# An S4 convolution and a gated GLU on one core: the hand-kept order of all work replaced by another

## The chip, the cores and the metric

The kernel runs on one core of a Trainium2 chip. The metric is device time in microseconds; the time of a kernel is the median of several runs. The profiles are of one execution each and count from the first to the last instruction (the span).

## What is computed

The input u has 2048 rows of 512 channels. Two branches work on it and are mixed by a gate per row:

```python
g = sigmoid((x * gate_w).sum(-1, keepdims=True))
# a: S4 convolution along the rows, one filter per channel
P = exp((dt * A)[:, :, None] * l)                  # 512 channels, 128 states, 2048 steps
K = einsum("dn,dnl,dn->dl", Cc, P, dB).real
a = irfft(rfft(u padded) * rfft(K padded))[:L] + u * Dskip
# b: gated GLU
b = (sigmoid(x @ w_gate) * (x @ w_up)) @ w_down    # 512 -> 1792 -> 512
return g * a + (1 - g) * b
```

## The kernel before

TensorE does two kinds of work. The wide products are the GLU: `gups` (line 1130, 1344 products of 128x512) are the hidden layer, and `dps` (line 1202, 672 products) the way down. Each float32 operand is split into a high and a low part, so three products stand for one. The small products are the convolution, done as a transform in two steps. They come in visits, each of one name:

- `ups` (line 742, 8 visits): first step of the transform of u. ScalarE copies the result to `evu`, and SyncE's queue writes it to `a_u` in memory (line 782).
- `kps` (line 653, 16 visits): the filter K, from the tables `B` (last operation on VectorE: line 590) and `T` (line 611). `B` and `T` have one buffer each. ScalarE copies the result to `kst`, and VectorE adds Dskip to it (line 670).
- `wps` (line 683, 8 visits): first step of the transform of K from the `kst` of two kps. ScalarE copies to `kev` (line 692), and SyncE writes `a_k` (line 698), one array for each half of the channels.
- `s2u`, `s2k` (lines 849 and 876, 8 visits each): second step, on `au` and `ak`, 1 MB each, read back from `a_u` and `a_k` (lines 819 and 828), with constants `wwu`, `wwk`. VectorE multiplies the two.
- `ips` (line 914, 8 visits) goes back; its result goes to `b_s` through `ev` (line 936).
- `fps` (line 990, 8 visits) is the last step, on `b_in` (line 977). The names `parts` are pieces of buffers that the first stage no longer needs and that hold au, ak, b_in and the sums in the second half.

The channels are done in two halves. The second half's s2u and s2k can't begin before the last kps and wps are done and written to memory. `sps` (line 409) is one product that spreads the gate's weights. The FFN's rows are done in two halves of 1024 as well; wide products remain until the end and are what TensorE does while the other work waits for memory.

Every strand of work is a generator that yields one step at a time: engine, cost, function, dependencies. `Plan.run` takes the next letter of the string `ORDER` (line 67 on; a letter stands for a kind of strand and an engine), and issues the next step of that kind. The string therefore sets the order of the instructions on every engine and on the DMA queues of SyncE and GpSimd; each engine works off its own in that order. The plan also keeps times of its own from cost figures (for a transfer so many KB, for a TensorE visit so many microseconds). They decide nothing on the chip but which free buffer is taken, and the semaphores come from the dependencies of the tiles.

Of the kernel before, what the change touches and what calls it, by code (L numbers as in the profile page):

```python
# [32 lines left out]
P = 128  # L33
L, D, F = 2048, 512, 1792
# [32 lines left out]
ORDER = (
    "ABEjDkhidDhEdHGDhjikddEjikIEDjkhddiEjkKZatatatdEdayzjktbFlDhiEjdyzAdkdddDhiEmedjkFydduzDhiLLMlNymMCOOPGDhdiydQOFRSdldmQE"
    "QQbZzezddQOTRyzejQWyddkWTWOWyTEjEzWdEWd0eeeTd1dOPQWEzWcWddjyyyUVVWkW0eeZdejdkvxxxW0exzvcLZx1xzWxaUeeaxzOEdUUyQWUWzFa1dWv"
    "xyQdRSTadWkExxxEyddRWtWX0YTtztQjvzTTUdtbxxxyseexeddQyyOVdVbZdUUzUUkRuj0e1leedScZQXyz0YdWzjTR1WkdseWGnovxedymWzjWeTdyddTk"  # L70
    "LTzdWkWzWWWxyzvyx1EUWEWdz0eedxFxy1xFxcedFZWjVzkWddldmWlmyyVUzUdxalmtUvxxaxx0ejvaxpqdaeeEUzyRSTdxqzje02yEtWddeeeeRTTEtWkd"
    "WWX0Y2tdrybxErTUseeededbMZzVNxMdOO02edejyeeVUPQOkUydUdQzUjRkScXZzEQz0YQQO2dTRseejQWydeneWTrjWWWWdkWdWWzvyzWxyeddzdWTv0ee"
    "eWTWdU1yEzky0eeeecdZOVVxoEWx0eeeeWzddWx2OPQdvjr2kOQQUExFUxly2UUzLRyduxSTFxkvWRmdWpxydadtzWXjkTTzFa0YlmxyTQlxFdylmUtsdzmd"
    "xeeyezadtjVxkQzxyLzeOVUExaEdj0qeUete2Uqer2r0dURyESTeeezyXed0YQb2jksR2dTbWzWedeeeTjZkckWdTy0eeWeWeWvxxxxEdUdV20eeZeexvWrx"
    "xxxWdcWVnW2WW0eejeezyWUUWUU2zWRSdyvx0eeeFFzoTdeWdRFWxlvpmrkdyzWWX2ldDDmD0YTyzTTxl2hdmiqsydehehUdMNizMOOeLxViPQOVUUUUdRSQ"
    "dx0DeQyzQXe2e0QOTRyddYQW2zWWsnodWqxrrrrOWTWyzThWOPWeedQdpWedTiWUxyWWOdqDDxWzWqrrr0edeVeyWzrVUUWUU0ddhyQDhQezdfRSf4566yzW"
    "hTRe2Wdd2e0QidyDhWeXiTieeizdy0YTTUQzfOf89%VVUUUdULdddseeQey2zX0dR%S2u2YdWyzWTRW%sndydW%WETef!EjkWFzeeTd02dTWUWyjWzWkW#&f"
    "ffdW&))))4VddVUWUEUeUWyzeeEdyzWR01e&&))))jdee01W5WfWeeSoe668pd0eeeq1TRWXq9rrEyzdyzk%r0YTT1TUdseyz%MddedV%NeMl%dOVydUjfd!"
    "#ydOPQjdOQQUUUXrzk0kQRSffEQO&YsddQeezWW1edEWWWjkEdWTRyzyjydTWnzd0eeejy&)dGW))WTzWkdzdm4)W0eeefdykWF1TUzOWEyz&dydWFoVWdVU"
    "UUjz&d)51))UOyfz668dRSlmy)lWdpWTdRkdyqqfrWdWzX90FzEY%TTTyzlyU1ddErrjkdyPmmQzseeee%Vd0e2eeeOEz%QVWUUU%!URdQ0e2eeeQXyQOdS0"  # L80
    "z2YTRQWWWWWW#fWWdjkyseeeeWdWEno&rdT&))))WTf40ee2eeTdUWj&k&5)jW)dy0ee2eedVfW))ffVd6zyWWzUU60Uep8UqEqRS2WTedeer9zdWXdRTydy"
    "0TYd%s%e%F%2!kerF#TU((dElm)z)))ydedejkrVzdVzddUUFyUlUXm0j&Y&Eyy))))jlrEdzkEkzmFsnopqqeedd$y$*jrzlmrdrrgy$f$+,*zzfydd-dy-"
    ",zfdzefy,k.z.e,3+--,ee45768g.ffef.e-,,3fE9%%%%ffgjd4d.ededj578e.,kEeyz3,E69%%%edegjff!.%fd.fed#((&ge)&)4k5376e)f)8g)E)f9"
    "yjy)z)k!f%e%edefd2%d3f#(&))&)&)d)ye4)56%e))6jfkd!8#$&&))))ee&()))$)9z3ykee%dd%%dyged%!e#&zzyg$$())))3d(())))ez*ed*+,zy-+"
    ",--zdyde-dFld$-zy--$z--F$dyd*+,dl$d*-d-yF$$--*-,+,..,elzme,..mzym$eeeeeee-z-3$3-e,33+yez,.,.e-ee,--g*--g-gee+3g,..,e-3ee"
    "-3-g--eeeee-g3ge3g")
# [243 lines left out]
def body(ctx, tc, xp, xt, prm, ldt, dsk, gw, wgu, wdn, c_wu, c_wf, c_wk, c_wwk, c_wwu, c_wwv, c_pw, out):  # L330
    nc = tc.nc
# [333 lines left out]
    def second(q, kss, kst, kready):  # L665
# [29 lines left out]
        te = []  # L695
        for x in range(4):
            dst, src = a_k[q // 4][q % 4, x], kev[32 * x:32 * x + 32]
            te.append((yield "SP", kb(215), lambda: S.dma_start(
                dst.rearrange("r l k d -> l r (k d)"), src.rearrange("p (r k) d -> p r (k d)", r=2)), [max(end)]))
# [72 lines left out]
    def urest(t4, e, i, ph, banks, tp):  # L772
        es, = yield EVU, 1
        ev = es.tile("evu")
        te = yield ("ACT", "DVE"), either(2 * D), lambda eng: copy(eng, ev, ph), [tp, es.t]
        banks.free(te)
        done = []
        for r in range(2):
            for h in range(2):
                dst = a_u[r, h, e, 4 * t4 + 2 * i:4 * t4 + 2 * i + 2].rearrange("j w g d -> g (j w) d")  # L780
                src = ev[64 * r + 32 * h:64 * r + 32 * h + 32].rearrange("p j (w d) -> p (j w) d", w=NW)
                done.append((yield "SP", kb(150), lambda: S.dma_start(dst, src), [te]))
        es.free(max(done))
# [6 lines left out]
    def passes():  # L790
# [11 lines left out]
        for j in range(NW):  # L802
# [9 lines left out]
            for p2 in range(4):  # L812
# [6 lines left out]
                ta.append((yield "SP", kb(520), lambda: S.dma_start(au.rearrange("p i g d -> p (i g d)"), src), [sa.t, rdone.t]))  # L819
# [43 lines left out]
    def kstep(wks, wwk, sk, ak, ready, both, tk):  # L863
# [6 lines left out]
        def mms():  # L870
            for i in range(2):
                for c in range(2):
                    for g_ in range(4):
                        for r in range(2):
                            q = slice(64 * r, 64 * r + 64)
                            mm(pk[i][32 * g_:32 * g_ + 32, r, c], wwk[q, i, g_, c], ak[q, :, i, g_], start=True, stop=True,  # L876
                               tile_position=(64 * r, 32 * g_), skip_group_check=True)
# [88 lines left out]
    def finals(j):  # L966
        yield bdone[j]
        yield E["wf"]
        for t4 in range(4):
# [4 lines left out]
            tb = []  # L974
            for q in range(2):
                src = b_s[j][:, :, q, 4 * t4:4 * t4 + 4].rearrange("c k j d -> (c k) (j d)")
                tb.append((yield "SP", kb(540), lambda: S.dma_start(b[:, q].rearrange("p j d -> p (j d)"), src), [sb.t, bdone[j].t]))
            plan.spawn(last(j, t4, b, sb, max(tb)), "last")

    def last(j, t4, b, sb, tb):  # L980
# [74 lines left out]
    def split(kind, src, hi, lo, slot, ready, n=512):  # L1055
# [4 lines left out]
        t = yield "SP", kb(0.55 * n), lambda: S.dma_start(flat if len(src.shape) == 2 else st, src), [s.t]  # L1060
# [239 lines left out]
```

## Time and profile before

| | |
|---|---|
| runs | 615.13, 615.53, 615.72 us; median 615.53 |
| the profiled execution | 617.09 us, its span 615.3 us |
| mean granted TensorE clock | 0.983 |
| wide products | 2016 |
| bytes moved by DMA | 104.19 MB, mean 169 GB/s |

A row of the view in order of time gives start, duration, engine, line, operation, tiles and count, and in brackets how long the engine stood idle before and who released it. Small products in float32 appear twice in the trace, so a visit of 64 has 128 records. In the windows each engine has its busy time and its instructions in brackets, and the last three columns are TensorE's granted clock, the share of DMA time and GB/s. SPq is SyncE issuing transfers.

### The profile page before, as it was taken

The numbers are of one execution on the slowest core, as the hardware profiler recorded it, in microseconds if no ns is written. First come the engines' busy times: TensorE is split into PE (matmuls) and PEld (weight loads), VectorE is DVE, ScalarE is ACT, GpSimd is POOL, SyncE is SP. The second block draws the span as 40 slices with busy tenths as digits, with TensorE's granted clock in tenths as the row PEclk, the third lists the DMA queues.
The fourth block names the chain that finished last, engine by engine and source line by source line (L and its number), as shares of the span: only waits on it lengthen the run. The fifth ranks groups of instructions, "written<-read, shape, count | busy, mean of one in ns | idle before, by whom it ended". The sixth has DMA issues, their size and how long they took to land.

```text
span 615.3 us, 16787 instructions
## 1 busy us (share of the span) xinstructions
PE 590.5 (96%) x7147; PEld 453.0 (74%) x7147; DVE 539.9 (88%) x765; ACT 414.8 (67%) x663; POOL 51.2 (8%) x80
## 2 busy tenths in 40 slices
PE   7999999999999999996999999999999988998997
PEld 3777777887778777884787778777777756676775
DVE  3899999999999997996899999999988566867897
ACT  3597979688798767995867878788957432231340
POOL 5000000010101111100110000001110022000031
PEclk7999999999999999997999999999999998999999
DMA  7612807562675586487518725444955799898776
GB/s 224 216 34 74 289 26 215 176 134 35 172 177 142 109 183 154 82 191 221 126 19 242 201 80 167 135 152 54 244 146 137 220 300 315 245 271 264 236 200 164
DMA packets 74156, 104.19 MB, mean 169 GB/s; under 512 B 7009, under 2 KB 45793, under 8 KB 73058
## 3 DMA queue, kind: packets, MB, share of 16 engines
q1 hardware_dynamic: 67170, 92.64, 49.9%
q0 software_dynamic: 6912, 10.49, 12.5%
q8 instruction: 56, 0.92, 0.6%
q14 instruction: 18, 0.15, 0.1%
HBM read 61.15 MB, written 41.95 MB: 168 GB/s over the span
## 4 chain that ended last, share of the span: by engine, by line
PE 75%; DMA 9%; issue 7%; DVE 3%; ACT 2%; SPq 1%; POOL 0%; DVEq 0%; ACTq 0%; POOLq 0%
PE gups L1130 40%; PE dps L1202 20%; PE kps L653 5%; PE s2k L876 3%; DMA ak<-a_k 2%; PE wps L683 2%; PE s2u L849 2%; PE ips L914 2%; PE ups L742 1%; DMA b_s<-ev 1%; DMA out<-part 1%; DMA st<-xt 1%; PE fps L990 1%; DMA wwk<-c_wwk 1%; DMA st<-wdn 1%
## 5 line engine op out<-in xcount | busy, mean ns | idle before, releaser
L1130 PE MATMUL gups<-x,gu 128*128 128x512 f32 x1344 | 334.7, 397 | 2.7 <-ACT x L1063 1.5
L1130 PEld LDWEIGHTS gups<-x,gu 128*128 128x128 f32 x1344 | 252.4, 190 | 69.6 <-issue 9.2
L1202 PE MATMUL dps<-dnw,h 128*128 128x512 f32 x672 | 172.7, 395 | 0.9 <-DVE h L1180 0.9
L1202 PEld LDWEIGHTS dps<-dnw,h 128*128 128x128 f32 x672 | 124.5, 188 | 36.9 <-issue 7.1
L1226 POOL DMA_DIRECT2D out<-part x32 | 28.3, 885 | 421.4 <-ACT part L1221 286.4
L581 ACT ACTIVATE B<-B 128x32 f32<-128x32 f32 (+2 forms) x96 | 53.9, 676 | 0.3
L1221 ACT ACTIVATE part<-dps,omg 128x512 f32<-128x512 f32 x48 | 32.8, 682 | 27.6 <-PE dps L1202 26.9
L1175 DVE SCALAR_TENSOR_TENSOR sg<-sg,gups 128x512 f32<-128x512 f32 x56 | 37.8, 680 | 9.8 <-ACT sg L1173 5.9
L1173 ACT ACTIVATE sg<-gups 128x512 f32<-128x512 f32 x56 | 33.0, 590 | 14.7 <-PE gups L1130 13.7
L1179 ACT ACTIVATE h<-sg 128x512 fp32r<-128x512 f32 x56 | 34.6, 622 | 11.3 <-DVE sg L1175 11.3
L609 DVE TENSOR_TENSOR t<-T,bz 128x1024 f32<-128x1024 f32 (+3 forms) x48 | 41.2, 859 | 0.6
L611 DVE TENSOR_TENSOR T<-T,t 128x1024 f32<-128x1024 f32 (+3 forms) x48 | 41.4, 863 | 0.3
L610 DVE TENSOR_TENSOR T<-T,bz 128x1024 f32<-128x1024 f32 (+3 forms) x48 | 41.3, 861 | 0.0
L1180 DVE TENSOR_TENSOR h<-sg,h 128x512 fp32r<-128x512 f32 x56 | 38.2, 685 | 2.5 <-ACT h L1179 2.4
L1064 DVE TENSOR_TENSOR gu<-st,gu 128x512 fp32r<-128x512 f32 (+1 forms) x50 | 32.9, 663 | 7.0 <-ACT gu L1063 7.0
L1063 ACT ACTIVATE gu<-st 128x512 fp32r<-128x512 f32 (+1 forms) x50 | 30.3, 607 | 12.0 <-DMA st<-wgu 11.9
L653 PEld LDWEIGHTS kps<-B,T 128*32 128x32 f32 x2048 | 29.9, 110 | 9.3 <-issue 6.7
L653 PE MATMUL kps<-B,T 128*32 128x64 f32 x2048 | 33.0, 220 | 2.1 <-issue 2.1
L355 ACT ACTIVATE ev<-ips 128x512 f32<-128x512 f32 x23 | 13.0, 594 | 30.9 <-PE ips L914 17.1
L499 ACT ACT_TABLE_LOAD x21 | 26.9, 1283 | 0.3
L692 ACT ACTIVATE kev<-wps 128x1024 f32<-128x1024 f32 x16 | 15.8, 1024 | 13.5 <-PE wps L683 13.3
L575 DVE TENSOR_TENSOR B<-pp,pw 128x1024 f32<-128x1024 f32 x16 | 19.6, 1224 | 4.9 <-PE kps L653 4.8
(124 smaller groups left out, 698.6 us busy)
## 6 DMA issues: line engine op xcount, KB each, us to landing
st<-wgu SPq DMA_DIRECT2D x46, 256.0 KB, 4.7
a_u<-evu SPq DMA_DIRECT2D x64, 128.0 KB, 3.8
a_k<-kev SPq DMA_DIRECT2D x32, 256.0 KB, 3.7
out<-part POOLq DMA_DIRECT2D x32, 256.0 KB, 4.7
b_s<-ev SPq DMA_DIRECT2D x64, 128.0 KB, 3.1
st<-wdn SPq DMA_DIRECT2D x25, 256.0 KB, 3.8
ak<-a_k SPq DMA_DIRECT2D x5, 1024.0 KB, 7.1
parts<-b_s SPq DMA_DIRECT2D x10, 512.0 KB, 6.1
```

Of the source, the lines that this page charges most:

```text
L581: A.activation(B[:, :, 0, 1 << k::2 << k], B[:, :, 0, 1:64 >> k:2], AF.Exp, scale=float(1 << k))
L609: yield "DVE", c, lambda: V.tensor_tensor(t2, src, sb, op=OP.mult), [t, slot.t]
L610: te = yield "DVE", c, lambda: V.tensor_tensor(dst, src, br, op=OP.mult), [t]
L611: te = yield "DVE", c, lambda: V.tensor_tensor(dst, dst, t2[:, :, ::-1], op=OP.add), [te]
L653: mm(p[32 * jj:32 * jj + 32, s], T[:, 32 * i + ch, c], B[:, ch, c], start=(c == 0), stop=(c == 1), tile_position=(0, 32 * jj), skip_group_ ...
L1064: te = yield "DVE", dve(n), lambda: V.tensor_tensor(lo, st, hi.bitcast(F32), op=OP.subtract), [te]
L1130: mm(p, gu[:, a, k, dc], x[:, b, dc], start=(dc + n == 0), stop=(dc == NC - 1 and n == 2))
L1173: t = yield "ACT", actp(512), lambda: A.activation(sg, pg_, AF.Tanh, scale=0.5), [tg, ss.t]
L1175: t = yield "DVE", dve(512), lambda: V.scalar_tensor_tensor(sg, sg, 1.0, pu, op0=OP.add, op1=OP.mult), [t, tu]
L1179: t = yield "ACT", act(512), lambda: A.activation(h[:, 0], sg, AF.Copy), [t, hs.t]
L1180: t = yield "DVE", dve(512), lambda: V.tensor_tensor(h[:, 1], sg, h[:, 0].bitcast(F32), op=OP.subtract), [t]
L1202: mm(p, h[:, a, 128 * s:128 * s + 128], dn[:, b], start=(f == fs[0] and n == 0), stop=(f == fs[-1] and n == 2))
```

## The change

All lines of `ORDER` are replaced by others. Besides, cost figures of the plan are changed: returns between kinds of TensorE work, one visit's length, and the KB that stand for transfers. No operation is added or removed.

```diff
-    "ABEjDkhidDhEdHGDhjikddEjikIEDjkhddiEjkKZatatatdEdayzjktbFlDhiEjdyzAdkdddDhiEmedjkFydduzDhiLLMlNymMCOOPGDhdiydQOFRSdldmQE"
+    "AEjkBEjkDhidDhiHdEjkdEjkDhIiddFEjkdlmDhGiddddEjkJZaatyddtaaDtzytubyhzDEejAEjikddzhFlkDhmyLidzeLddMiNMCODhiFdyOddPQOzdEld"
...
-            c = n + (0.0 if mode == self.last else 0.09 if self.last == "f" else 0.21 if mode == "f" else 0.1)
+            c = n + (0.0 if mode == self.last else 0.18 if self.last == "f" else 0.33 if mode == "f" else 0.2)
...
-        t = yield "PE", ("f", 0.95, 4), lambda: mm(p[:, 0], warm[:1, :P], row, start=True, stop=True), [t, bank.t]
+        t = yield "PE", ("f", 1.95, 4), lambda: mm(p[:, 0], warm[:1, :P], row, start=True, stop=True), [t, bank.t]
...
-            te.append((yield "SP", kb(215), lambda: S.dma_start(
+            te.append((yield "SP", kb(295), lambda: S.dma_start(
...
-                ta.append((yield "SP", kb(520), lambda: S.dma_start(au.rearrange("p i g d -> p (i g d)"), src), [sa.t, rdone.t]))
+                ta.append((yield "SP", kb(1010), lambda: S.dma_start(au.rearrange("p i g d -> p (i g d)"), src), [sa.t, rdone.t]))
...
-                tk.append((yield "SP", (kb(740), 0.2), lambda: S.dma_start(ak.rearrange("p o i g d -> p o (i g d)"), src), [sk.t, kdone[j].t]))
+                tk.append((yield "SP", (kb(1130), 0.2), lambda: S.dma_start(ak.rearrange("p o i g d -> p o (i g d)"), src), [sk.t, kdone[j].t]))
...
-        t = yield "PE", ("64x32", 1.57, 129), mms, [tk] + [b.t for b in banks]
+        t = yield "PE", ("64x32", 1.68, 129), mms, [tk] + [b.t for b in banks]
```

Six more transfers have their KB changed (a_u and b_s writes 150 to 139, b_in 540 to 485, the GpSimd writes of the last step 215 to 230, the loads of weights and x 0.55 to 0.52 per column).

The following rows show the order at three places. TensorE from the last wps ahead of the first s2u to that s2u, before:

```order
L683 MATMUL wps<-wk,kst 64x128 x64
L1202 MATMUL dps<-dnw,h 128x512 x3
L1130 MATMUL gups<-x,gu 128x512 x12
L1202 MATMUL dps<-dnw,h 128x512 x3
L1130 MATMUL gups<-x,gu 128x512 x6
L1202 MATMUL dps<-dnw,h 128x512 x6
L1130 MATMUL gups<-x,gu 128x512 x12
L1202 MATMUL dps<-dnw,h 128x512 x3
L1130 MATMUL gups<-x,gu 128x512 x6
L849 MATMUL s2u<-au,wwu 32x256 x32
```

The same place now:

```order
L683 MATMUL wps<-wk,kst 64x128 x64
L1202 MATMUL dps<-dnw,h 128x512 x6
L1130 MATMUL gups<-x,gu 128x512 x18
L1202 MATMUL dps<-dnw,h 128x512 x3
L1130 MATMUL gups<-x,gu 128x512 x6
L1202 MATMUL dps<-dnw,h 128x512 x6
L1130 MATMUL gups<-x,gu 128x512 x6
L1202 MATMUL dps<-dnw,h 128x512 x9
L1130 MATMUL gups<-x,gu 128x512 x18
L849 MATMUL s2u<-au,wwu 32x256 x32
```

Between wps and s2u there were 51 wide products, and there are 72 now. The first s2u came behind 999 wide products of the kernel and comes behind 990 now.

SyncE's queue at that s2u, with the a_k writes of this wps ahead, before:

```order
L698 DMA a_k_60<-kev 32x2x1024 x4
L1060 DMA st<-xt 128x512
L815 DMA wwu<-c_wwu 128x256
L819 DMA au<-a_u 128x2048
L1060 DMA st<-xt 128x512
L824 DMA wwk<-c_wwk 128x512
L828 DMA ak<-a_k_60 128x16x128
```

The same place now:

```order
L698 DMA a_k_60<-kev 32x2x1024 x4
L1060 DMA st<-xt 128x512
L815 DMA wwu<-c_wwu 128x256
L819 DMA au<-a_u 128x2048
L824 DMA wwk<-c_wwk 128x512
L1060 DMA st<-xt 128x512
L828 DMA ak<-a_k_60 128x16x128
```

The second load of xt stood between au and wwk and stands behind wwk now.

TensorE from the last kps to the second half's first s2u, before:

```order
L653 MATMUL kps<-B,T 32x64 x64
L1130 MATMUL gups<-x,gu 128x512 x6
L683 MATMUL wps<-wk,kst 64x128 x64
L1202 MATMUL dps<-dnw,h 128x512 x6
L1130 MATMUL gups<-x,gu 128x512 x18
L990 MATMUL fps<-b_in,wf 32x256 x16
L1130 MATMUL gups<-x,gu 128x512 x24
L1202 MATMUL dps<-dnw,h 128x512 x6
L990 MATMUL fps<-parts,wf 32x256 x16
L1202 MATMUL dps<-dnw,h 128x512 x6
L849 MATMUL s2u<-parts,wwu 32x256 x32
L1202 MATMUL dps<-dnw,h 128x512 x6
```

The same place now:

```order
L653 MATMUL kps<-B,T 32x64 x64
L683 MATMUL wps<-wk,kst 64x128 x64
L1130 MATMUL gups<-x,gu 128x512 x12
L990 MATMUL fps<-b_in,wf 32x256 x16
L1130 MATMUL gups<-x,gu 128x512 x24
L1202 MATMUL dps<-dnw,h 128x512 x3
L1130 MATMUL gups<-x,gu 128x512 x6
L990 MATMUL fps<-b_in,wf 32x256 x16
L1130 MATMUL gups<-x,gu 128x512 x18
L849 MATMUL s2u<-parts,wwu 32x256 x32
L1130 MATMUL gups<-x,gu 128x512 x6
L1202 MATMUL dps<-dnw,h 128x512 x3
```

The row after the first piece is s2k; after the second come six gups and then s2k. The last kps stood behind 1638 of the 2016 wide products and stands behind 1590 now; wps followed it after six gups and follows at once; from wps to s2k there were 66 wide products and are 78. On SyncE the four a_k writes of this wps were issued one after the other, with a load of 256 KB and two of 512 KB (`parts<-out`, `parts<-b_s`) between them and ak; now two loads of b_in, 512 KB each, stand between the second and the third a_k write.

More of the change, by code (lines that the diff above doesn't have):

```diff
@@ L72 @@
[L72 to L75, printed above, removed]
@@ new lines @@
+    "1aQjQaTadyWRkWXtzdEQ0zvxxExxTTtTdQjYUsdtzdV1tbeeVUUUUuXykzddejyyd0dYEyOjlQdR1zWkzSWWTRzdWkbZWEWsevxxxeemW0deyzWjWdTjedeT"
+    "TUkcZ0WdeeFFyzx1ydvxxxdeVzddWGxkFWyzydWzVUUvx0xylmlmxxEedcZadzlmyeezdaEaUUyzedWRWtkSvxxxadv0noEeeyWt2eeddTRWWxdtjTpWXtb0"
+    "2TYdyqTUjzMbZseeeedVNMOOdxVUd10ee2eexLxx1dyPQOUUqrrUXykcZQQR02YQESQTzdOseeeeRQdvxxxxWkWWWvxxcZzxT0eeeeWzxOWTWjOWWWkTyzjd"
+    "0eeeedvyU2PQWdWzOEWVydVQkWdW0eUUedeaydznjdxdFFldEajUxQxWvyUlW2oRSyddFeTzzxmarEzdFRxkLyzyjTxWmxErdTylpaWXx0YtlQkzTddzyUdd"
@@ new lines @@
+    "2tkzseedmtQ2jtmyzOuVykzeEVeUq0UdUEeeee0d2eeUXRSjQTeeqrbRbZ202dyTYszWrWWWWcZEeWnoTdeWTWUWkyWevxxxxrzWWre02dVeeeWe0V2UUvxx"
+    "UdxxeeUeceRd0WEvxWjySTxe2RedeWveWj0TdeWFWGeeTepXxzlm0YjTkyxFskddyUlMqdzeNmkzddVMOOVPQydyDDFDdLUzddedOqrrlDrxrQzUymUzxeQh"
+    "ihUXQ2iRSQxd0YOyzTRhihdQWsnoTWLWyedOWOWTWWTP2WWzWxUiW2Wpqeqrre0rdydQdOeWrzWVdVUUUyQeedU0eDhQffeedzy42fdRSzd5QT2Wdy0edeR6"
+    "zDWeTf268yTWDdWhWXzii0YT9yz2UQO%VVUUUUsddhyeeeddX%RS02YsT%dQeeedyWR%WiWDf!hiWno0WWzeTWze#fedT&T&UdyWWzdWd2EE)))y0ezVWde)"
@@ new lines @@
+    "ff4WVUUUWUjke01dF&&eRS)WWjeyze566))f8W)ddpETRWyzWdqqrdyzTWX019%TyTdYUEzkjkMsuVN%2MdyzVedOOUee01dddPQUOEjkUUededeyzXydQ%Q"
+    "dRSrE01YQfEQOlEy%!QWdTjzWrOOWRWkWWzWsnodjkW#fWey&&)f)4))eejkT0ddeTdreezWdTUPyWWmWzWyzQOd01&ed&)f)e1V5VUWU6e0Ed1jdQyzkUe6"
+    "epyzWU)WdRSQdFyzldqjkfeyzqr89WdrTRd%rWX%yzdTyzEFfd0QTTYmFWUQ)dysed%ljdzyVe%zVE!#mlmyjz&U&f1e))))e0UUUXdkeeefe0RS2kdOT4R&"
+    "QYsWWWWdWnoWWW&)T)rTT5e)eed2E6edff60eWy2UVVd8eWpqeWWzWWeyEqrdrfrU0UzUU9%RST)%W%Reed2ed%rEWW!eyd0eeeej02dWXeeekTT2e0T#(&Y"
@@ new lines @@
+    "2dyzy))))UsezjeVFdeedVk&(UUdUdydUlzXFm0Yzsnoyjkp))))qq2$$*FyEEFdd+,rdr$yd$dderdrf*+ff4z-z-,f,.yd.djkfl,j,.f,zd-5zmy-dz,,"
+    "6ylye68dzmzyf4k9dedfEfz%%dyl.jd%5Ezfm6.ky78%gE.,zd!9%de3,f.%j.f4dy%zeefde#(&(y&fEgf)))g)ejd))))5ff6k%fjk783d9%%%dyeez!de"
+    "edfg3#(&(&)e))Eezygg))4)E5ekeg)7%689$)3e$g%de%%zee!dyjk#&(&3f%)()))d!dee*)#$eejkd)))($*3dyee(e))()z()zye3+,z)+ded-Fyz--l"
+    "ddy))---),e-FelF-dmd--$lm$*+,-ddye--$$*-,,$$..,*d++3zyme,.,ee-zd.-3dzye-z-,,dey-z-$$ee-3*e+..-,y-ee,.3e-z-.ee3---eee3eee"
@@ L88 @@
+    "e3--ege3gggggee3gg")
 XLATE = 0
@@ L781, in urest @@
                 src = ev[64 * r + 32 * h:64 * r + 32 * h + 32].rearrange("p j (w d) -> p (j w) d", w=NW)
-                done.append((yield "SP", kb(150), lambda: S.dma_start(dst, src), [te]))
+                done.append((yield "SP", kb(139), lambda: S.dma_start(dst, src), [te]))
         es.free(max(done))
@@ L935, in evict @@
                 src = ev[64 * r + 32 * c:64 * r + 32 * c + 32]
-                end.append((yield "SP", kb(150), lambda: S.dma_start(dst, src), [max(te)]))
+                end.append((yield "SP", kb(139), lambda: S.dma_start(dst, src), [max(te)]))
         es.free(max(end))
@@ L976, in finals @@
                 src = b_s[j][:, :, q, 4 * t4:4 * t4 + 4].rearrange("c k j d -> (c k) (j d)")
-                tb.append((yield "SP", kb(540), lambda: S.dma_start(b[:, q].rearrange("p j d -> p (j d)"), src), [sb.t, bdone[j].t]))
+                tb.append((yield "SP", kb(485), lambda: S.dma_start(b[:, q].rearrange("p j d -> p (j d)"), src), [sb.t, bdone[j].t]))
             plan.spawn(last(j, t4, b, sb, max(tb)), "last")
@@ L1022, in last @@
                 t = 4 * t4 + k[i]
-                done.append((yield "POOL", kb(215), lambda: nc.gpsimd.dma_start(out[t, :, cols], y[:, i], accum_op=OP.add), [max(t1), begun[t]]))
+                done.append((yield "POOL", kb(230), lambda: nc.gpsimd.dma_start(out[t, :, cols], y[:, i], accum_op=OP.add), [max(t1), begun[t]]))
                 begun[t].set(done[i])
@@ L1059, in split @@
         st = flat if len(hi.shape) == 2 else flat.rearrange("p (a b) -> p a b", a=hi.shape[1])
-        t = yield "SP", kb(0.55 * n), lambda: S.dma_start(flat if len(src.shape) == 2 else st, src), [s.t]
+        t = yield "SP", kb(0.52 * n), lambda: S.dma_start(flat if len(src.shape) == 2 else st, src), [s.t]
         def halves():
```

15 lines of the change are left out of this document (1 added, 14 removed).

## The prediction

> **What bounds the kernel now.** I read the page first, then the chain of waits, then TensorE, VectorE and SyncE in order of time at each place where TensorE stood still. Page, parts 1 and 4:
>
> ```profile
> span 615.3 us, 16787 instructions
> PE 590.5 (96%) x7147; PEld 453.0 (74%) x7147; DVE 539.9 (88%) x765; ACT 414.8 (67%) x663; POOL 51.2 (8%) x80
> PE 75%; DMA 9%; issue 7%; DVE 3%; ACT 2%; SPq 1%; POOL 0%; DVEq 0%; ACTq 0%; POOLq 0%
> ```
>
> TensorE is the bound, VectorE close behind. The amount of TensorE work is fixed: 2016 wide products (gups and dps, 128x512) and 64 visits of small ones (ups, kps, wps, s2u, s2k, ips, fps). Their prices, from the chain of waits (start, us, what):
>
> ```profile
> 358.24 4.08 PE gups L1130 x18
> 366.69 1.92 PE kps L653 x128
> 368.61 2.94 PE gups L1130 x12
> ```
>
> A wide product takes 4.08/18 = 0.227 us. The twelve after a visit take 2.94 instead of 2.72, so coming back costs 0.22. The order can change only idle time, clock and the number of these returns (two visits side by side need one). The longest idle time, TensorE in order of time (start, us, what, idle before), and the chain of waits behind it:
>
> ```profile
> 266.46 2.10 PE L683 MATMUL wps<-wk,kst 32*64 32x128 f32 x128
> 268.49 0.97 PE L1202 MATMUL dps<-dnw,h 128*128 128x512 f32 x3
> 285.72 2.37 PE L849 MATMUL s2u<-au,wwu 32*32 32x256 f32 x64 [5.36 <-DMA wwk<-c_wwk]
> ...
> 285.74 2.35 PE s2u L849 x64
> 288.09 1.58 PE dps L1202 x3
> 289.67 3.62 PE gups L1130 x12
> ```
>
> And SyncE's queue ahead of it (start, us from issue to issue end):
>
> ```profile
> 270.96 2.77 SPq L698 DMA_DIRECT2D a_k<-kev  x4
> 275.51 1.56 SPq L815 DMA_DIRECT2D wwu<-c_wwu  x1
> 277.13 0.44 SPq L819 DMA_DIRECT2D au<-a_u  x1
> 279.57 0.33 SPq L1060 DMA_DIRECT2D st<-xt  x1
> 279.94 0.66 SPq L824 DMA_DIRECT2D wwk<-c_wwk  x1
> ```
>
> The first s2u needs au (1 MB), issued 10.7 us after wps began; it begins 17.2 us after wps ended (268.49). Only 51 wide products, 11.6 us, stood in between. The stall has a second price, seen in the windows (after the busy columns: granted clock, DMA share, GB/s):
>
> ```profile
> 279.00:291.00 12.00, 6.64 (x78) 4.27 (x77) 6.15 (x7) 5.04 (x9) 0.00 (x0) 0.73 0.69 205
> 285.00:286.00 1.00, 0.28 (x16) 0.31 (x32) 0.00 (x0) 0.00 (x0) 0.00 (x0) 0.50 0.57 193
> ```
>
> At half clock s2u takes 2.35 instead of 1.5 (503.47 to 504.97 below), the three dps 1.58 instead of 0.90, the twelve gups 3.62 instead of 2.72: 2.4 more. Stall and clock: 5.4 + 2.4 = 7.8. VectorE stood still 12 - 6.15 = 5.85 in the same stretch.
>
> The second place is the first read of the filter table's second half:
>
> ```profile
> 479.27 1.99 PE L653 MATMUL kps<-B,T 128*32 128x64 f32 x128
> 501.19 1.67 PE L1202 MATMUL dps<-dnw,h 128*128 128x512 f32 x6
> 503.47 1.58 PE L849 MATMUL s2u<-parts,wwu 32*32 32x256 f32 x64 [0.60 <-issue]
> 504.97 1.67 PE L1202 MATMUL dps<-dnw,h 128*128 128x512 f32 x6
> 509.27 3.21 PE L876 MATMUL s2k<-ak,wwk 64*32 64x256 f32 x64 [2.63 <-DMA ak<-a_k]
> 532.50 0.97 PE L1202 MATMUL dps<-dnw,h 128*128 128x512 f32 x3
> 534.01 2.01 PE L849 MATMUL s2u<-parts,wwu 32*32 32x256 f32 x64 [0.54 <-ACT ev L355]
> 554.21 1.66 PE L1202 MATMUL dps<-dnw,h 128*128 128x512 f32 x6
> 557.60 1.96 PE L876 MATMUL s2k<-parts,wwk 64*32 64x256 f32 x64 [1.73 <-ACT ev L355]
> ...
> 488.25 2.77 SPq L698 DMA_DIRECT2D a_k<-kev  x4
> 489.75 4.75 DMA a_k<-kev
> 495.41 13.73 DMA ak<-a_k
> 510.00:511.00 1.00, 1.00 (x31) 0.80 (x23) 0.87 (x2) 0.00 (x0) 0.00 (x0) 0.50 1.06 445
> ```
>
> Six dps should take 1.36 + 0.22. They reach the next visit after 2.28 (501.19 to 503.47) and 4.30 (504.97 to 509.27): 0.7 + 2.7 lost; s2k at half clock takes 3.2 instead of 1.96, and I add 0.3 for the products behind it: 4.9 in all. By the same sum the six dps from 554.21 lose 1.8 and the three from 532.50 0.6. These 7.3 us can go.
>
> **Who decides when the last kps comes.** VectorE builds its operands B and T (VectorE in order of time; then its window from 20 to 478.66):
>
> ```profile
> 477.44 1.22 DVE L590 TENSOR_TENSOR B<-B,ex 128x1024 f32<-128x1024 f32 x1
> 478.58 0.68 DVE L1064 TENSOR_TENSOR dnw<-st,dnw 128x512 fp32r<-128x512 f32 x1
> 479.18 0.68 DVE L1180 TENSOR_TENSOR h<-sg,h 128x512 fp32r<-128x512 f32 x1
> 20.00:478.66 458.66, 431.95 (x604) 0.99 0.56 143
> ```
>
> B is done 0.61 us before kps begins. So removing TensorE's idle time alone is not enough: VectorE must also come earlier.
>
> **The change.** The edited planner costs are not executed on the chip; the string is. The rows of the order stand in the section on the change: the last kps moves from behind 1638 wide products to behind 1590; wps is put directly behind it; from wps to the first s2k of the second half there are 78 wide products instead of 66; from the wps ahead of the first s2u to that s2u 72 instead of 51; and on SyncE the xt load that waited 2 us for a buffer no longer stands between au and wwk.
>
> *Start.* The second w load now goes out ahead of the first x, and sps comes after 9 products instead of 12. The first window:
>
> ```profile
> 0.00:20.00 20.00, 16.56 (x39) 9.10 (x40) 8.36 (x19) 7.27 (x13) 9.12 (x32) 0.74 0.73 240
> ```
>
> 3.4 us of idle and a mean clock of 0.74: the first product may come half a microsecond later and the second chunk of weights no longer waits behind a third x. I cost it at nothing, within 1 us either way; the half clock covers a late load.
>
> *First s2u.* 72 wide products are 16.3 us, with one return 16.5, against the 17.2 that au needed: 0.7 left of 5.4, no half clock. Gain 7.1. Bounds: 7.8, or nothing if au is issued 5 us later in its row.
>
> *Returns.* Seven pairs of visits touch ahead of the last kps instead of five: 2 x 0.22 = 0.45 gained; behind it two more, 0.4. But wps directly behind kps must wait for ScalarE to copy kst and VectorE to correct it, which the six gups covered: 1.0 lost (at most the 1.4 of those six gups, which were enough; I take 1.0).
>
> *Last kps.* TensorE alone would reach it at 479.27 - 48 x 0.227 - 7.1 - 0.45 = 460.8. VectorE: its order up to that B has seven operations fewer (three sg, h, gu, dnw, gwb) at 0.60 apart (478.58 to 479.18) = 4.2, and 5.35 of the 5.85 idle goes with the stall: 479.27 - 4.2 - 5.35 = 469.7. The rest of its idle time, 458.66 - 431.95 - 5.85 = 20.9 us, is waits for TensorE and ScalarE that a new order may shrink. Between these ends I take the middle, 465: no row says which.
>
> *From there to the end.* How long a read of ak takes, from the answer on that tile:
>
> ```profile
> DMA to landing us min/median/max: 5.4/7.1/13.7
> ```
>
> Before, 615.3 - 479.27 = 136.0. Now 48 wide products more, + 10.9; the 7.3 goes. Part comes back: the new order puts two b_in loads between the four a_k writes, and b_in waits for the first fps, so the last a_k goes out some 6 us after wps, lands 4.75 later, and ak, issued then at 11, lands at 18 by the median and 24.7 by the longest. TensorE gets to s2k after 78 x 0.227 + two fps and an s2u (3.5) + returns 0.9 = 22.1. The wait is 0 to 2.6; I take 1.0. Then + 1.0 for kst and - 0.4: 136.0 + 10.9 - 7.3 + 1.0 + 1.0 - 0.4 = 141.2. Total 465 + 141.2 = 606.2 of span.
>
> The profiled execution lasted 617.09 with a span of 615.3; the timed runs, 615.53 in the median. So a span goes to the median with + 0.2: **606.4**.
>
> At both stalls the trace shows half clock, after 5.36 and after 2.63 us of idle. [...]
>
> **The rivals.**
> *A. VectorE keeps up and all waits go:* 460.8 + 141.2 - 1.0 + 0.2 = 601.2. For: VectorE has 20.9 us of idle time to recover. Against: the last B ends only 0.61 us ahead of its kps now.
> *B. The second half's reads are late again:* the write-to-read chain (a_k, then ak) loses the 4.9 once more: 606.4 + 4.9 = 611.3. For: the two b_in loads in SyncE's queue. Against: 12 wide products more of cover.
> *C, slower. VectorE is the bound and does not come earlier:* the last kps needs VectorE's B. If its idle time does not fall by the 5.35, kps comes at 475.1, TensorE waits for it in pieces, and 475.1 + 141.2 + 0.2 = 616.5; with B's 4.9 on top 621.4. It decides from 475.3 on (616.7). For: kps moves ahead by 10.9 us of TensorE's work, but by only 4.2 of VectorE's.
> *D. No net move:* waits shift, 615.5 within 1.2.
>
> **The numbers.** Forecast 0.62, A 0.12, B 0.09, C 0.12, D 0.05. The likeliest case runs from 602 (TensorE's end) to 611 (VectorE's). The range goes down to 599 (A with a little more) and up to 615, which leaves out C and part of D. A difference of 0.2%, 1.2 us, is about what a measurement of this kernel can tell from no change. Faster 0.83, same 0.05, slower 0.12.
>
> **What would show it.** Right: no idle row above 2 us before the first s2u, clock 1.00 from 20 us on; the last kps near 465, with VectorE's B just ahead of it; 141 us from there to the end. The first step is wrong if s2u again waits 5 us for au. The VectorE step is wrong if kps shows idle time before it and comes after 472, or has B done many microseconds earlier. The last step is wrong if s2k waits for ak, or the tail behind the last fps is longer than now.

## The result, and the profile after

The changed kernel takes 598.81 us in the median of four runs (598.72 to 599.98), the kernel before 615.33 (613.40 to 615.72): a ratio of 0.974, with 0.972 to 0.977 as its 95% interval. That is 16.5 us less. The forecast was 606.4, so faster came true, and the time lies 0.2 us below the low end of the range; by the ratio, on the 615.53 that the forecast started from, it is 599.6, just inside. The profiled execution took 598.84 with a span of 597.1. The page after, parts 1 and 4:

```profile
span 597.1 us, 16787 instructions
PE 584.2 (98%) x7147; PEld 450.6 (75%) x7147; DVE 539.5 (90%) x767; ACT 409.8 (69%) x658; POOL 50.6 (8%) x80
PE 64%; DVE 19%; ACT 6%; issue 4%; DMA 4%; SPq 2%; DVEq 0%; ACTq 0%
```

VectorE's busy time is as it was (539.9 before), TensorE's is 6.3 us shorter, and the chain of waits now runs through VectorE for 19% of the span (3% before). The places that the prediction named, TensorE in order of time:

```profile
273.32 1.49 PE L849 MATMUL s2u<-au,wwu 32*32 32x256 f32 x64 [0.17 <-DMA wwk<-c_wwk]
456.44 1.99 PE L653 MATMUL kps<-B,T 128*32 128x64 f32 x128
459.37 0.43 PE L683 MATMUL wps<-wk,kst 32*64 32x128 f32 x5 [0.94 <-DVE kst L670]
461.34 3.35 PE L683 MATMUL wps<-wk,kst 32*64 32x128 f32 x123 [1.53 <-issue]
481.77 1.50 PE L849 MATMUL s2u<-parts,wwu 32*32 32x256 f32 x64
495.10 1.49 PE L849 MATMUL s2u<-au,wwu 32*32 32x256 f32 x64
498.11 1.96 PE L876 MATMUL s2k<-parts,wwk 64*32 64x256 f32 x64
```

The first s2u waits 0.17 instead of 5.36 and runs at full clock (1.49). The last kps comes at 456.44 instead of 479.27. The kst wait behind it is there, and the rest of wps waits 1.53 more for nothing that the profile shows. In the second half no s2u and no s2k carries an idle time of any size. The windows of the start, of the way to the last kps, and of the half clock behind it:

```profile
0.00:20.00 20.00, 16.79 (x53) 10.19 (x54) 10.87 (x23) 9.90 (x20) 8.46 (x32) 1.00 0.76 252
20.00:456.44 436.44, 433.17 (x5390) 341.46 (x5388) 424.02 (x592) 357.22 (x564) 28.00 (x32) 1.00 0.58 149
460.78:464.19 3.41, 2.85 (x109) 2.85 (x115) 0.68 (x2) 0.00 (x0) 0.00 (x0) 0.50 0.82 300
```

And the second of these for the kernel before, up to its last kps:

```profile
20.00:479.27 459.27, 449.15 (x5451) 354.46 (x5449) 432.56 (x605) 368.62 (x583) 27.11 (x31) 0.99 0.56 143
```

VectorE stood still for 459.27 - 432.56 = 26.7 us on the way to the last kps and stands still for 436.44 - 424.02 = 12.4 now. TensorE stood still for 459.27 - 449.15 = 10.1 us and stands still for 436.44 - 433.17 = 3.3 now. The first window has a clock of 1.00 where it had 0.74. So 22.8 us were gained up to the last kps. TensorE's window accounts for most of them: it holds 61 products fewer (48 of them by the order, the rest because more are done before 20 us), which are 13.8 us, and 6.8 us less idle time. From there to the end 140.7 us pass instead of 136.0, with 48 wide products (10.9) more in them.

### The profile page after: what moved, and what is told of

Same layout as the page of the kernel before. It is cut to its first block, busy times and chain, and to the rows that moved or that the text cites. A ratio compares the mean times of both kernels' runs of the same rounds, so it can differ in the third digit from the quotient of the medians.

```text
span 597.1 us, 16787 instructions
## 1 busy us (share of the span) xinstructions
PE 584.2 (98%) x7147; PEld 450.6 (75%) x7147; DVE 539.5 (90%) x767; ACT 409.8 (69%) x658; POOL 50.6 (8%) x80
## 4 chain that ended last, share of the span: by engine, by line
PE 64%; DVE 19%; ACT 6%; issue 4%; DMA 4%; SPq 2%; DVEq 0%; ACTq 0%
PE gups L1130 31%; PE dps L1202 20%; PE kps L653 4%; PE wps L683 2%; PE s2k L876 2%; DVE T L610 2%; PE s2u L849 2%; DVE t L609 2%; DVE T L611 2%; DMA au<-a_u 2%; DVE h L1180 1%; DMA wwk<-c_wwk 1%; PE fps L990 1%; PE ips L914 1%; DVE sg L1175 1%
## 5 line engine op out<-in xcount | busy, mean ns | idle before, releaser
L355 ACT ACTIVATE ev<-ips 128x512 f32<-128x512 f32 x20 | 11.3, 593 | 24.7 <-PE ips L914 14.5
L508 ACT ACTIVATE af<-ex 128x1024 int32<-128x1024 f32 x16 | 16.9, 1056 | 11.0 <-DVE ex L559 11.0
```

## The experiments

Single executions of one kernel lay up to 11 us apart on the two chips used here (the kernel before: 609.7 to 621.1), so each ratio to the kernel before is given with its interval. The changed cost figures have no run of their own; the first kernel below has them with the old order behind a new start, and its ratio of 0.9991 leaves them nothing that these runs can tell. A string put together from two takes the first letters of the one, then the other without the letters already used. Two of the kernels with the old order keep the old figures (the later s2u, and the new head); all others below carry the changed ones, which only decide which of several free buffers is taken.

### The start

In the first profiles the first kps begins at 72.75 us before and at 68.08 now. These 4.67 us lie ahead of all that the prediction had put a price on; the start it had costed at nothing. Is that the order?

```diff
-ORDER = (the old string)
+ORDER = (the first 45 letters of the new string, then the rest of the old one)
```

> The kernel before with only the start of the new order (the first 45 letters: second w load ahead of the first x, sps after 9 products; from the first dps on the old order). Theory T (the order of the first loads decides whether TensorE runs at half clock from 8.5 to 18.7 us; TensorE is the bound, so what is lost there is lost for good): granted clock 1.00 in the first 20 us and the time 4.6 us under before, 610.7. Rival W (half clock at the start is a matter of the single run, not of the order): clock about 0.74 as before and 615.3 within 1. Rival V (VectorE sets the last kps and does not follow): clock 1.00, but the last kps still near 479 and the time 615 within 1.

```diff
-ORDER = (the new string)
+ORDER = (the first 80 letters of the old string, then the rest of the new one)
```

> The changed kernel with the old start (the first 80 letters of the old order). Theory T: half clock for some 10 us, the last kps near 461 and 603.4. Rival W: clock 1.00 and 598.8 within 1. Rival V: half clock but the last kps still near 456.4, 599 within 1.

Measured: the old kernel with the new start 614.55 us, ratio 0.9991 (0.9955 to 1.0026); the new kernel with the old start 598.1, ratio 0.9727 (0.9678 to 0.9775). Neither start moves the time. The first window of four kernels, in this order: new start on the old order, old start on the new order, old start on the old order (the third experiment), new start on half of the new order (the fourth):

```profile
0.00:20.00 20.00, 16.55 (x57) 9.89 (x58) 11.79 (x24) 10.67 (x19) 9.89 (x32) 1.00 0.76 255
```

```profile
0.00:20.00 20.00, 16.69 (x59) 10.21 (x60) 11.63 (x23) 10.48 (x19) 9.53 (x32) 1.00 0.79 253
```

```profile
0.00:20.00 20.00, 16.51 (x58) 10.05 (x59) 11.30 (x23) 9.95 (x17) 10.18 (x32) 1.00 0.76 250
```

```profile
0.00:20.00 20.00, 16.78 (x46) 9.73 (x47) 10.44 (x22) 9.23 (x18) 8.46 (x32) 0.83 0.76 250
```

The old start has full clock twice here, and the new one has lost it once. Theory T falls. W holds in this, that the half clock at the start differs between executions and not with the order (for the first kernel it had expected 0.74, and 1.00 came); the profile of before happened to have 10 us of it. V is not settled by these two: both had full clock at the start, and in the first the last kps came at 476.74, 2.5 us earlier than before and not near 479.

Of the 4.67 us, the half clock is some 3.0: the kernel with the later s2u, which has the instructions of before up to the first kps and a clock of 1.00, begins it at 69.74. The other 1.7 come with the order behind the start, since the new kernel with the old start has its first kps at 68.08 too.

### The first s2u alone

```diff
-...fRSf4566yzWhTRe2Wdd2e0QidyDhW...
+...fRSf4yzWhTRe2Wdd2e0Qid566yDhW...
```

Letter 5 is the s2u on TensorE, 6 its two copies; d are six gups each, e three dps.

> The kernel before with only its first s2u moved behind 24 more wide products (75 behind wps instead of 51). Theory T: its wait falls from 5.36 to under 0.5, no half clock there, and 7 us less: 608.3. Rival V (VectorE stood still 5.85 us there and must come earlier too for the last kps): the wait goes but comes back in pieces ahead of the later kps, 612 to 615. Rival M (the read of au is slow for what SyncE has queued, whatever the place of s2u): the wait stays over 3 us, 613 to 615.

Measured: 609.94, ratio 0.9911 (0.9876 to 0.9947), 5.5 us less. TensorE in order of time:

```profile
282.31 1.50 PE L849 MATMUL s2u<-au,wwu 32*32 32x256 f32 x64
289.02 1.99 PE L653 MATMUL kps<-B,T 128*32 128x64 f32 x128 [1.59 <-ACT part L1221]
338.73 1.96 PE L876 MATMUL s2k<-ak,wwk 64*32 64x256 f32 x64 [1.89 <-issue]
437.18 1.58 PE L849 MATMUL s2u<-au,wwu 32*32 32x256 f32 x64 [2.23 <-DMA b_s<-ev]
504.51 1.96 PE L876 MATMUL s2k<-ak,wwk 64*32 64x256 f32 x64 [2.66 <-DMA ak<-a_k]
```

The wait and the half clock are gone, as T said: M is out. T's 7 us lie within the interval. The 1.5 that are short may be the waits that are new or larger here (1.59, 1.89, and 2.23 for 1.39); they are for ScalarE, for nothing shown and for a transfer, not for VectorE's B, as V would have it.

### The two halves of the string

```diff
-ORDER = (the old string)
+ORDER = (the first 1096 letters of the new string, then the rest of the old one)
```

> The new order up to behind the first s2u, the old one from there (all kps, wps and s2u visits behind it stand where they stood before: last kps behind 1638 wide products). Theory T (stages add up: 4.65 from the start, 7.3 from the first s2u, the last kps near 467.3, then 136 as before): 603.5. Rival V (VectorE can't bring B 12 us earlier with 48 wide products' worth of extra hidden work ahead of the last kps; its idle time behind the stall was 10.3): last kps after 470 and 606.5 to 612. Rival F (the old rest depends on the old lateness, its reads come later relative to TensorE now): 606 to 609 with new waits in front of s2u and s2k.

```diff
-ORDER = (the new string)
+ORDER = (the first 1090 letters of the old string, then the rest of the new one)
```

> The counterpart of the third kernel: the old order up to behind the first s2u, the new one from there (last kps behind 1590 wide products, wps next to it). Theory A (what the two halves of the order bring adds up: new head alone took 6.2 off, the whole 16.2): 615.4 minus 10 is 605.4, with the first s2u still waiting about 5 us and no wait over 0.6 ahead of the second half's s2k. Rival F (the new rest needs the new head: it comes late and its reads with it): over 610. Rival H (all of the gain sits in the first s2u and behind the last kps: 7 and 6): 609 to 610.

(The third kernel in it is the one above, with the new head.)

Measured: new head and old rest 609.25, ratio 0.9896 (0.9838 to 0.9954); old head and new rest 613.74, ratio 0.9965 (0.9930 to 1.0000). They bring 6.2 and 1.3 us, together 7.5 of the 16.5. TensorE in the first of the two:

```profile
336.54 1.96 PE L876 MATMUL s2k<-ak,wwk 64*32 64x256 f32 x64 [1.81 <-issue]
434.09 1.59 PE L849 MATMUL s2u<-au,wwu 32*32 32x256 f32 x64 [1.33 <-DMA au<-a_u]
471.30 1.99 PE L653 MATMUL kps<-B,T 128*32 128x64 f32 x128
501.27 1.96 PE L876 MATMUL s2k<-ak,wwk 64*32 64x256 f32 x64 [2.67 <-DMA ak<-a_k]
```

And in the second:

```profile
282.49 2.37 PE L849 MATMUL s2u<-au,wwu 32*32 32x256 f32 x64 [4.69 <-DMA wf<-c_wf]
293.23 3.11 PE L653 MATMUL kps<-B,T 128*32 128x64 f32 x128 [3.01 <-ACT part L1221]
424.90 1.58 PE L849 MATMUL s2u<-au,wwu 32*32 32x256 f32 x64 [2.40 <-DMA au<-a_u]
```

F's new waits are there both times, with 609.25 a little above its 606 to 609 and 613.74 over its 610. In the first kernel V's figures are met as well (a last kps after 470, and 606.5 to 612), but not its reason: from 20 us to that kps TensorE stands still for 6.6 us in all and VectorE for 21.6. Its start ran at half clock for 6.83 us (the 0.83 of its first window above). An estimate of what that cost is half of it, 3.4 (the 10.24 us of before cost some 3.0), and T's 467.3 with these is 470.7. In the second kernel A and H are out. Each half keeps the waits that its own old part has and gets new ones at the seam and behind it. The gain belongs to the string as a whole: these two halves of it do not add up to it.

### Which engine sets the last kps

The next two kernels, and the first of the section behind them, were run beside the changed kernel itself.

> The changed kernel once more, as the measure for the three that follow on the same chip: 598.8 within 1.5. If half clock at the start is a matter of the single run, some of its runs are 3 to 4 us longer at a lower mean clock; if the order decides it, none is.

Measured: 599.28, ratio 0.9740 (0.9674 to 0.9806); its profiled execution had the longest time of the four, 602.81, with the last kps at 458.30. But for the very end it ran at half clock from 285.70 for 3.41 us and from 463.20 for 6.83, and the first profile of the same kernel from 460.78 for 3.41 alone: the half clock is a matter of the single run.

```diff
-            yield "DVE", c, lambda: V.tensor_tensor(t2, src, sb, op=OP.mult), [t, slot.t]
+            def first():
+                for _ in range(2 if e == 16 and i == 0 else 1):
+                    V.tensor_tensor(t2, src, sb, op=OP.mult)
+            yield "DVE", c, first, [t, slot.t]
```

> The changed kernel with 8 more VectorE operations, one at the last doubling of each table T: the product of 128x1024 that is written to t is formed twice (1.14 each, 9.1 us in all, the same result). Theory T (TensorE is the bound up to the last kps; VectorE's 12.4 us of idle time between 20 and 456 take most of it): 0 to 3 us more, 599 to 602. Rival V (VectorE sets each kps, its idle time is not to be had): 9 us more, 608.

Measured: 603.99, ratio 0.9831 (0.9776 to 0.9885), 4.7 more in the medians. The last kps in order of time, and the window up to it:

```profile
460.70 1.99 PE L657 MATMUL kps<-B,T 128*32 128x64 f32 x128
20.00:460.70 440.70, 433.24 (x5386) 339.65 (x5384) 432.17 (x600) 355.95 (x562) 28.00 (x32) 1.00 0.58 148
```

Against the first profile VectorE is 8.2 us busier (432.17 for 424.02) and idles 8.5 us instead of 12.4; kps comes 4.3 later. Against the changed kernel beside it (423.5 busy, 14.8 idle, kps at 458.30) it comes 2.4 later. So a quarter to a half of the addition shows, and idle time takes the rest: well under V's 9, and in the medians over T's 3. Not all of the 4.3 need be VectorE's, since waits of TensorE of the kind in the next section are 3.0 us in this window and 1.1 in the first profile. The intervals just overlap, so the size is the profile's more than the medians'.

```diff
                                 for n, (a, b) in enumerate(((0, 0), (0, 1), (1, 0))):
+                                    if half == 0 and 1 <= f <= 10 and dc + n == 0:
+                                        mm(p, gu[:, a, k, dc], x[:, b, dc], start=True, stop=True)
                                     mm(p, gu[:, a, k, dc], x[:, b, dc], start=(dc + n == 0), stop=(dc == NC - 1 and n == 2))
```

> The changed kernel with 40 more wide products on TensorE in the first half of the hidden layer (the first product of a group formed twice, f from 1 to 10; 40 times 0.227 is 9.1 us; the result stays the same), all ahead of the last kps. Theory T: 9.1 us more, 607.9. Rival V (VectorE sets the last kps, TensorE would otherwise wait for it): 0 to 3 us more, 599 to 602. If both this and the VectorE kernel cost 4 us or more, the two engines run in step and the bound changes hands from place to place.

Measured: 618.81, ratio 1.0059 (1.0025 to 1.0094): 19.5 us more, though 40 products are 9.1. No theory had that. That this and the VectorE kernel both cost over 4 us was to show two engines in step; it cannot, for the 19.5 hold something else. The last kps comes at 475.41, 19.0 later than in the first profile. Of these 9.1 are the products, 6.2 are idle time of TensorE (9.47 us from 20 us on, for 3.27), and some 3.4, by the same estimate, are half clock for twice 3.41 us, from 191.40 and from 218.70. VectorE stands still for 31.1 us on that way, so it is not what holds kps back. Most of the idle time is in waits that the changed kernel does not have (in each row the records behind the wait):

```profile
132.68 0.42 PE L653 MATMUL kps<-B,T 128*32 128x64 f32 x13 [1.13 <-issue]
191.19 0.94 PE L653 MATMUL kps<-B,T 128*32 128x64 f32 x30 [2.54 <-issue]
218.35 1.75 PE L742 MATMUL ups<-u,wu 32*32 32x512 f32 x23 [1.83 <-issue]
249.15 0.55 PE L653 MATMUL kps<-B,T 128*32 128x64 f32 x25 [1.19 <-issue]
```

They lie within a visit, and the profile shows nothing that they wait for. The next section counts their places in TensorE's stream of instructions.

### wps and the instruction stream

```diff
-...XFm0Yzsnoyjkp))))qq2$$*FyEEFdd+...
+...XFm0Ydzsnoyjkp))))qq2$$*FyEEFd+...
-                ok = sorted((s for s in r[0] if not s.held), key=lambda s: s.t)[:r[1]]
+                ok = sorted((s for s in r[0] if not s.held), key=lambda s: s.t - (1.0 if s.tag is None and s.pool.slot.tag == "kev0" else 0.0))[:r[1]]
```

Y is the last kps, p its wps; the second edit keeps every buffer as it was.

> The changed kernel with six gups between the last kps and its wps, as it was before; every other instruction and buffer stays in its place. Theory P (wps next to kps costs its wait for kst, 0.94, the 1.53 behind it and the half clock that follows, about 1.4 in wps and the next gups): up to 3.9 us less, 595 to 597.9. Rival Q (the 1.53 is not tied to kst and comes again wherever wps stands; only 0.94 goes, and the one return that the pair saved, 0.22, comes back): 598 to 598.6.

Measured: 598.79, ratio 0.9742 (0.9683 to 0.9801), no difference that these runs can tell from the changed kernel beside it; the interval is too wide to shut out the times of P. The trace decides for Q's condition: the wait for kst is gone, and the other wait stands in the gups now. TensorE in order of time, first of the changed kernel run again, then of this one:

```profile
463.94 3.47 PE L683 MATMUL wps<-wk,kst 32*64 32x128 f32 x116 [2.28 <-issue]
```

```profile
460.60 0.50 PE L1130 MATMUL gups<-x,gu 128*128 128x512 f32 x1 [2.27 <-issue]
```

Another instruction waits, for the same time. Counted from the program's start, in matrix products and weight loads together, both rows are behind instruction 11148. Counted so, all such waits of over 0.4 us inside a visit fall on a few places:

| kernel | instructions ahead of the wait (its length, us) |
|---|---|
| before | 4782 (1.35), 9112 (0.57), 11404 (1.08) |
| changed | 4524 (0.46), 6050 (0.66), 11148 (1.53) |
| changed, run again | 6050 (2.15), 11148 (2.28) |
| wps after six gups | 6050 (0.89), 11148 (2.27) |
| 8 more VectorE operations | 3506 (0.91), 6050 (0.91), 10128 (1.18), 11148 (1.81) |
| 40 more products | 2228 (1.13), 3506 (2.54), 4016 (1.83), 4780 (1.19), 6560 (1.14), 9872 (0.43), 11404 (2.42) |

From 2228 to 3506 are 5 x 256 - 2, to 4016 another 2 x 256 - 2, to 4780 another 3 x 256 - 4, to 6050 another 5 x 256 - 10, from 11148 to 11404 exactly 256. The few missing are semaphore instructions of TensorE, which the traces hold too. With them counted, all 49 such waits in the 14 traces of this case stand 192 or 193 instructions past a multiple of 256. Part 3 of the page of the changed kernel has a queue named `instruction`:

```profile
q8 instruction: 56, 0.92, 0.7%
```

TensorE's 14294 instructions are 55.8 times 256, and there are 56 packets, 0.92 MB in all, 16 KB each. One of them, from 459.08 to 460.04, lies at the beginning of the wait that ends at 461.34 (DMA in the window from 459 to 461):

```profile
q8 instruction: 1, 0.02, 3.0%
```

The same holds for the others: in 48 of the 49 waits TensorE goes on 1.2 to 1.6 us after the end of such a packet, and in the last one 0.7 us after it.

So theory I was made, an inference from these counts and times, as no view shows what a packet holds: TensorE waits at a boundary of 256 instructions for the next block of its program, which has not come where the 256 before ran within a few microseconds. The test shifts all of them with 44 (then 12) more instructions at the very start:

```diff
-    for _ in range(WARM):
-        mm(spin, warm.bitcast(BF16)[:, :P], warm.bitcast(BF16), start=True, stop=True)
+    for _ in range(31):
+        mm(spin[:, :148], warm.bitcast(BF16)[:, :P], warm.bitcast(BF16)[:, :148], start=True, stop=True)
```

> The changed kernel with 31 short products (148 columns) in place of the 9 of 512 at the very start, while TensorE has nothing else to do: 44 instructions more, the same columns, every later instruction in its old order but 44 places further on in TensorE's stream. Theory I (the gaps that the profile calls issue come at every 256th instruction of TensorE, when the 256 before it ran in less than 3 to 5 us): all such gaps move 44 instructions forward in the program; the one of 1.5 to 2.3 us in the last wps (10 instructions in) falls into the kps ahead of it or shrinks to about 1, 1 to 3 us less: 596 to 598. Rival J (a gap belongs to its place, to wps behind kps): the same gap at the same wps, 599 within 1.

> The same with 15 products of 308 columns: 12 instructions more. Theory I, with 3 us as the shortest time for 256 instructions before 455 us and 4.8 after, worked through the measured order: gaps of 8.6 us in all where the changed kernel has 6.7 and the one shifted by 44 has 4.4: 600 to 602. Rival J: 599 within 1.

> The kernel with six gups between the last kps and wps, shifted by 44 instructions too. Theory I: gaps of 3.9 in all, no wait for kst: 2 to 4 us under the changed kernel, 595 to 597.5, the fastest of all. Rival J: 598.8 as without the shift.

Measured: shifted by 44, 610.12, ratio 0.9913 (0.9884 to 0.9942); by 12, 603.28, ratio 0.9819 (0.9766 to 0.9872); wps later and 44, 608.25, ratio 0.9888 (0.9839 to 0.9937). The changed kernel has 0.9740 (0.9674 to 0.9806), so the shift by 44 costs some 10 us with not one product moved against another (the two ran on different chips, each beside the kernel before). The waits in it:

```profile
130.20 0.33 PE L653 MATMUL kps<-B,T 128*32 128x64 f32 x9 [1.64 <-issue]
185.57 0.43 PE L653 MATMUL kps<-B,T 128*32 128x64 f32 x16 [1.62 <-issue]
210.98 1.86 PE L742 MATMUL ups<-u,wu 32*32 32x512 f32 x5 [2.73 <-issue]
243.41 0.32 PE L653 MATMUL kps<-B,T 128*32 128x64 f32 x7 [1.04 <-issue]
475.20 0.54 PE L683 MATMUL wps<-wk,kst 32*64 32x128 f32 x17 [2.44 <-issue]
```

They stand behind 2228, 3506, 4016, 4780 and 11404 instructions: the very places of the kernel with 40 more products, which are other products in this one. J falls, and the place is as I says; that the wait is for a block stays the inference it was. The size was forecast with the wrong sign: I had assumed 3 us as the least time for 256 instructions before 455 us (and 4.8 behind it, in the forecast for the shift by 12), and a gain from it; no trace shows such a least time. The blocks ahead of the first four of these waits ran in 2.2 to 2.7 us. The kernel with wps later waits at the same five places, 11.6 us in all where 3.9 were forecast. Shifted by 12, the forecast came nearer: 603.28 for 600 to 602, and 7.5 us of waits for 8.6, behind 3506 (2.36, which the profile puts down to VectorE, though such a packet lands 1.4 us before the wait ends), 6050 (1.65) and 11148 (3.48). The five waits are 9.5 us, against 4.4 in the changed kernel beside the others. Some of the 10 us is not theirs. The first window of the shifted kernel, then of the changed one run again:

```profile
0.00:20.00 20.00, 17.20 (x65) 12.42 (x66) 9.75 (x22) 8.74 (x16) 9.40 (x32) 1.00 0.77 255
```

```profile
0.00:20.00 20.00, 16.33 (x56) 9.72 (x57) 11.57 (x23) 10.53 (x21) 9.66 (x32) 1.00 0.76 253
```

Without the products ahead of the work, 65 - 31 = 34 are done by 20 us instead of 56 - 9 = 47: 13 x 0.227, 3.0 us lost at the start. What these short products do there was not separated from the shift. No version beat the changed kernel by more than the runs can tell.

## Why the prediction was right in sign and too small

*The first s2u.* Right: 0.7 of 5.36 was to be left, 0.17 is; the half clock went. Done alone it gains 5.5 in the median, and the interval (3.3 to 7.6) holds the 7.1.

*The last kps.* This step failed: "Between these ends I take the middle, 465: no row says which." It came at 456.44. The end of TensorE alone, 460.8, was the right one, as TensorE's window says: only 3.3 of its 436.44 us up to that kps are idle. The sum for TensorE is 4.4 us above this and 2.5 above the changed kernel run again, and some 3.0 is the half clock at the start that its execution had. The old order with full clock there, the first kernel of the experiments, reaches its last kps here,

```profile
476.74 1.99 PE L653 MATMUL kps<-B,T 128*32 128x64 f32 x128
```

and 476.74 - 10.9 - 7.1 - 0.45 = 458.3. The changed kernel run again has it there:

```profile
458.30 1.99 PE L653 MATMUL kps<-B,T 128*32 128x64 f32 x128
```

That the two agree to the last digit is luck, for the first profile of the same kernel has it 1.9 us earlier.

VectorE's bound of 469.7 counted 20.9 us of its idle time as fixed but for what new waits might shrink; in fact idle time fell from 26.7 to 12.4, over half of it. That B is done just ahead of kps did not show VectorE to be the bound: it is done 0.42 us ahead of the last kps now (456.02), with TensorE hardly idle. B has one buffer, so VectorE in turn waits for kps before it begins the next (4.6 us in all on the page after). The added VectorE work shows the same, since half of it or more disappears.

*The start.* Costed at nothing, and the order of the start indeed does nothing there. But the sum was made on an execution that had lost 3.0 at half clock. The step from span to median, + 0.2, took 1.56 of that out (617.09 - 615.53); an ordinary execution needs + 1.7 (598.81 - 597.1).

*From the last kps to the end.* Forecast 141.2, measured 140.7. The waits of the second half went; 0.94 for kst stands against 1.0. Not seen: the 1.53 behind it and 3.41 us at half clock. Not needed: the 1.0 for a late ak, as no s2k waits. Nor did the sum see that a wait of 1.08 within the old wps would go. What was missed on both sides nearly cancels, and that the forecast is within 0.5 is in part luck.

*Together.* 606.4 - 8.6 (last kps) - 0.5 (the end) + 1.5 (span to median) = 598.8. Rival A, with a chance of 0.12 and a time of 601.2, came nearest, in its time and in its reason; B and C did not occur.

## What to carry to other kernels

An engine that finishes just ahead of the one that waits is not the bound before it is known what it waited for itself: sum its busy time, not its idle time, and test with added work. Sum from more than one execution where the clock differs from run to run. TensorE's place in its own instruction stream was a cost of its own here: 9.5 us of waits in the kernel shifted by 44, against 4.4 in the changed kernel run again. And an order that is tuned as a whole cannot be priced, or taken over, part by part.

## What the hardware showed

**Blocks of instructions.** In the 14 traces TensorE waits 0.4 to 3.5 us inside a visit 49 times, each time 192 or 193 instructions past a multiple of 256. The 256 instructions before these waits ran in 2.2 to 5.0 us, but not every block that ran so fast is followed by one: in the kernel before, the 256 from 425.92 us on ran in 2.5 us without it. The 56 packets of the queue `instruction`, 16 KB each, are as many as the blocks of 256 in TensorE's 14294 matrix products and weight loads (55.8); in the kernel before, the waits end 1.39, 1.23 and 1.30 us after such a packet. A trace has 2 to 7 such waits for its 56 packets, and they come to 4.4 us in the changed kernel run again, 9.5 shifted by 44, and 11.6 with wps later and 44. What starts such a packet, and how long ahead of the boundary, was not measured.

**Clock in windows.** But for those cut off by the end of a run, all stretches of half clock here last 3.41, 6.83 or 10.24 us, multiples of one length. Two of the longer ones, at the start of the kernel before and behind the last kps of the changed one run again:

```profile
8.08:18.32 10.24, 9.68 (x20) 5.65 (x19) 5.91 (x13) 2.92 (x6) 4.03 (x13) 0.50 0.94 316
```

```profile
463.20:470.02 6.82, 6.08 (x129) 5.27 (x130) 0.11 (x1) 2.34 (x3) 0.00 (x0) 0.50 0.33 114
```

Within a run they begin whole multiples of 3.413 us apart: in the kernel before at 8.08, 284.56 and 509.84, which are 81 and 66 such lengths from one to the next: 276.48 / 81 = 225.28 / 66 = 3.413.

What counts in these traces is TensorE's idle time within one window, a stretch of this length on this grid. Laid out so, the 14 traces have 2438 windows that began at full clock. Half clock followed each of the 29 with more than 2.0 us idle, none of the 2396 with less than 1.68, and 5 of the 13 between. How long it then lasts, one window or up to three, this does not say.

So waits of nearly the same length cost clock in one kernel and not in another. The s2k of the second half shows it. It waited 2.52 us in the old order with the new start, 2.66 in the kernel with the later s2u and 2.67 in the one with the new head. In the first, the whole wait lies in one window, which leaves TensorE 0.89 us busy, and the next is at half clock:

```profile
504.21:507.62 3.41, 0.89 (x23) 0.46 (x29) 1.31 (x3) 1.43 (x3) 1.61 (x2) 1.00 1.16 326
507.62:511.03 3.41, 3.41 (x58) 2.08 (x43) 2.95 (x3) 0.00 (x0) 0.14 (x1) 0.50 1.05 383
```

In the other two it is split over two windows, neither with 2.0 us idle, and the clock stays full:

```profile
500.07:503.48 3.41, 1.78 (x18) 1.05 (x6) 2.52 (x3) 2.38 (x4) 0.72 (x2) 1.00 1.16 306
503.48:506.90 3.42, 2.38 (x66) 1.79 (x67) 1.67 (x2) 0.07 (x1) 1.54 (x2) 1.00 1.09 386
```

```profile
497.07:500.48 3.41, 1.53 (x6) 0.92 (x6) 2.46 (x3) 2.45 (x4) 0.67 (x2) 1.00 1.16 301
500.48:503.90 3.42, 2.63 (x67) 1.99 (x68) 1.89 (x3) 0.00 (x0) 1.30 (x2) 1.00 1.12 388
```

So it is at the start too: the five profiles with half clock there have 1.69 to 2.49 us of the first waits in one window, the other nine at most 1.85. No run moved a wait against the grid on purpose.
